# Forming the block sums of a mixing matrix by accumulating DRAM transfers instead of GpSimd adds, in a two-layer attention and gMLP kernel

## The chip, the cores and the metric

The kernel runs on one core of one Trainium2 chip. The metric is the device time of one execution in microseconds (us). Before the change it was measured three times: the median is 1361.53 us, the lowest 1360.88 and the highest 1361.72.

The core has a matrix engine (TensorE, PE in the profile, with its weight loads as PEld), a vector engine (VectorE, DVE), an activation engine (ScalarE, ACT), GpSimd (POOL) and SyncE (SP), which in this kernel only issues DMA transfers. Each engine works off its own instructions in program order: an instruction that waits holds back all that stand behind it on that engine. PEq, SPq and POOLq are the sequencers of these engines, on which their DMA issues are shown.

## What is computed

Two layers, each made of a linear-attention block and a gated mixer block, on 2048 tokens of 512 features, all in float32:

```python
x = x + _A_ref(_layernorm(x), wqkv, wo)                 # linear attention, 32 heads of 16
x = x + _B_ref(_layernorm(x), w_in, w_sp, b_sp, w_out)  # gMLP
x = x + _A_ref(_layernorm(x), wqkv, wo)                 # the same weights again
x = x + _B_ref(_layernorm(x), w_in, w_sp, b_sp, w_out)

# _B_ref
z = gelu(einsum("bsd,df->bsf", x, w_in))                # 2048 x 1792
z1, z2 = z[..., :896], layernorm(z[..., 896:])
g = einsum("ts,bsf->btf", w_sp, z2) + b_sp[None, :, None]
return einsum("bsf,fd->bsd", z1 * g, w_out)

# _A_ref: phi(t) = where(t > 0, t + 1, exp(t)) + 1e-6
num = einsum("bhqd,bhde->bhqe", phi(q), kv)
den = einsum("bhqd,bhd->bhq", phi(q), z)[..., None] + 1e-6
```

The change concerns `w_sp`, the 2048 x 2048 mixing matrix. It depends on no activation, so what is formed from it can be formed at any time.

## The kernel before

**Products.** Every float32 product is made of three matmuls on operands split into a high and a low part (`mm3`, lines 147 to 151; `acc`, lines 1615 to 1621; `nested_mm`, lines 1550 to 1553). ACT makes the high part with a copy (`high`, line 135), DVE the low part with a subtraction (`low`, line 138).

**Block sums.** The product with `w_sp` is done by a Strassen-like scheme with seven products in place of eight. It needs, beside blocks of the matrix, four sums of blocks: S1 = A21 + A22, S3 = A21 + A11, S2 = S1 + A11 and S4 = S2 + A12. Each block has 8 row slabs k (0 to 7), and each slab two halves j of 128 x 512 numbers (256 KB). The sums are kept in DRAM, one tile `s{m}_{k}` of 512 KB for each sum m and slab k, 32 tiles in all. They are made once, during layer one, and read in both layers by `P4.fetch` (line 1415) ahead of the products P6 (S2), P7 (S3), P5 (S1) and P3 (S4).

**How they are made.** The class `Sums` does it half slab by half slab: 16 first units (three raw pieces are loaded by SP, GpSimd makes three adds at line 1209, three sums are stored at line 1202) and 16 fourth units (S2 and A12 are loaded, one add, one store). That is 64 adds of 128 x 512. `TOKEN_TICKS` puts seven of the first units into the steps of `P2.run` (SP loads into z tiles of which the tag is free, line 1195; SP stores), and `MIX_TICKS` puts the other 25 units into the mixing steps of `P4.run` (SP loads into page slots, GpSimd issues the stores).

**Order of the work in layer one.** The order is written out by hand:
- `P1.first`, steps s = 1 to 17: layer norm, K and Q projections and the matrix G for each of 16 token tiles.
- `transition`, the change of halves: the attention's small matrices, and the first token tiles of the next part (`p2.a(0)` to `p2.a(3)`, line 793, a multiplication on GpSimd; `a2_den` on DVE at line 805; `a2_mul` at line 814).
- `P2.run`, steps s = 1 to 18: the attention output (`c`, DVE add `c2` at line 846), the second layer norm, its turning through DRAM, and the two halves of `w_in` (`e` and `f`).
- `P4.run`, steps g = 0 to 61: the mixing products (`mm`), each step fetching the matrix part of step g + 4.
- then the output projection, which runs into layer two.

**The norm of a token tile in `P2.run`.** `c_stats` takes the statistics on DVE (lines 264 and 266). GpSimd makes rs and nb of them in three small instructions (lines 268, 269, 273). `c3` normalises on ACT (line 279) with nb. On ACT the late part of phi(q) stands behind that (lines 417 and 418), on DVE its last instruction (line 419), and behind this on DVE the add `c2` (line 846), the low part of the next token tile (line 138) and the statistics of the tile after (264, 266). A token tile's attention operand (`qt`) goes to DRAM and comes back rearranged (SP, lines 315 and 131), and DVE transposes it in 32 x 32 blocks (line 330).

**Queues.** All loads and nearly all stores are issued by SP, in program order. Each of SP's DMA issues also waits until the eighth issue before it has landed, and GpSimd's are guarded in the same way among themselves.

## Time and profile before

| | |
|---|---|
| median of three runs | 1361.53 us |
| time of the profiled execution | 1361.72 us |
| its span, first to last instruction | 1360.0 us (1.72 us lie around it) |
| PE busy | 1353.4 us |
| DVE busy | 1034.1 us |
| ACT busy | 638.1 us |
| POOL busy | 496.3 us |
| PE's granted clock | 1.00 throughout |
| bytes moved by DMA | 310.18 MB, 228 GB/s on the mean |

How to read the views: a row of a timeline gives the start in us from the span's start, the duration in us, engine, source line, operation, the tile written and the tiles read by their program names without numbers, and in brackets how long the engine had been idle before and what ended that. "x4" merges four in a row. A row of the waits gives the waiting instruction, what it waited for, then the total in us, the number of times and the longest. A row of stretches gives the busy time of each engine with its number of instructions, then PE's clock, the share of time in which the 16 DMA engines were busy, and what they moved. A row of DMA issues ends with the number of issues, the size of each and the median time from issue to landing. "L1202" is line 1202 of the kernel before. In the changed kernel lines below the edits have other numbers: 793 becomes 806, 846 becomes 859, 1202 and 1204 are the new transfers.

### The profile page before, as it was taken

To read this page: it belongs to the slowest core of one execution; us is meant where nothing else is said; L and a number is where in the kernel's file an instruction comes from. 1 tells how busy PE (TensorE), PEld (TensorE's weight loads), DVE (VectorE), ACT (ScalarE), POOL (GpSimd) and SP (SyncE) were. 2 spreads that over 40 slices of the span, in tenths; PEclk is the share of its full clock that TensorE was granted. 3 is DMA by queue.
4 is the path that set the end of the run, shared out by engine and by line. 5 is a ranking of instruction groups with operands and counts; after the bars stand their busy time and mean duration, and the time that the engine had idled before them with its cause. 6 is when DMAs were issued, how large, how long until landed. Compare 5 with 4: busy or idle time off the path is not lost.

```text
span 1360.0 us, 18353 instructions
## 1 busy us (share of the span) xinstructions
PE 1353.4 (100%) x6087; PEld 1133.3 (83%) x6087; DVE 1034.1 (76%) x1582; ACT 638.1 (47%) x1021; POOL 496.3 (36%) x594
## 2 busy tenths in 40 slices
PE   9999999999999999999999999999999999999998
PEld 7888888888888888888888888888888888888887
DVE  7985898776866789985678768877768798978642
ACT  6875544446443342532456655443556434533310
POOL 2333376533284248427321134533230011412340
PEclk9999999999999999999999999999999999999999
DMA  5773478976797988886876524666568798568652
GB/s 182 238 210 93 124 263 295 303 238 186 235 353 266 310 285 277 265 345 201 252 227 214 178 83 127 203 220 204 187 205 278 225 335 318 198 200 304 224 184 88
DMA packets 181744, 310.18 MB, mean 228 GB/s; under 512 B 15696, under 2 KB 67920, under 8 KB 177552
## 3 DMA queue, kind: packets, MB, share of 16 engines
q1 hardware_dynamic: 166544, 251.45, 57.1%
q0 software_dynamic: 11504, 51.12, 10.4%
q10 hardware_dynamic: 3600, 6.42, 1.3%
q8 instruction: 48, 0.79, 0.2%
q14 instruction: 48, 0.39, 0.1%
HBM read 211.68 MB, written 97.26 MB: 227 GB/s over the span
## 4 chain that ended last, share of the span: by engine, by line
PE 95%; DVE 3%; ACT 1%; issue 0%; POOL 0%; DVEq 0%; ACTq 0%; POOLq 0%
PE bank L151 17%; PE bank L149 17%; PE bank L150 17%; PE bank L1620 9%; PE bank L1619 9%; PE bank L1621 9%; PE bank L1552 4%; PE bank L1550 4%; PE bank L1553 4%; PE bank L995 1%; PE bank L994 1%; PE bank L993 1%; PE bank L736 1%; PE bank L512 0%; DVE pg L138 0%
## 5 line engine op out<-in xcount | busy, mean ns | idle before, releaser
L1621 PE MATMUL bank<-qd,pg 128*128 128x512 f32 x544 | 211.9, 390 | 0.0
L1620 PE MATMUL bank<-qd,pg 128*128 128x512 f32 x544 | 211.9, 390 | 0.0
L1619 PE MATMUL bank<-qd,pg 128*128 128x512 f32 x544 | 211.9, 390 | 0.0
L1466 DVE TENSOR_TENSOR qd<-qd,qd 128x1024 fp32r<-128x1024 f32 x104 | 140.4, 1350 | 65.2 <-ACT qd L1457 64.9
L1457 ACT ACTIVATE qd<-qd 128x1024 fp32r<-128x1024 f32 x104 | 110.1, 1059 | 132.0 <-DMA qd<-s 39.3
L151 PE MATMUL bank<-qd,pg 128*128 128x512 f32 x380 | 148.7, 391 | 0.4 <-DVE pg L138 0.4
L135 ACT ACTIVATE pg<-pg 128x512 fp32r<-128x512 f32 (+1 forms) x146 | 89.4, 620 | 125.0 <-DVE pg L330 46.3
L268 POOL TENSOR_SCALAR rs<-mv 128x1 f32<-128x1 f32 x95 | 42.2, 444 | 260.3 <-DVE mv L266 250.7
L1641 POOL TENSOR_TENSOR bg<-bg,pg 128x512 f32<-128x512 f32 x56 | 89.8, 1614 | 108.2 <-DMA pg<-z 98.8
L1620 PEld LDWEIGHTS bank<-qd,pg 128*128 128x128 f32 x544 | 102.2, 188 | 21.2
L1619 PEld LDWEIGHTS bank<-qd,pg 128*128 128x128 f32 x544 | 102.2, 188 | 21.2
L1621 PEld LDWEIGHTS bank<-qd,pg 128*128 128x128 f32 x544 | 102.2, 188 | 21.0
L138 DVE TENSOR_TENSOR pg<-pg,pg 128x512 fp32r<-128x512 f32 (+1 forms) x143 | 106.0, 742 | 16.3 <-ACT pg L135 12.9
L1209 POOL TENSOR_TENSOR pg<-pg,pg 128x512 f32<-128x512 f32 x50 | 80.2, 1604 | 101.9 <-DMA pg<-in_wsp_dram 68.7
L149 PE MATMUL bank<-qd,pg 128*128 128x512 f32 x284 | 111.0, 391 | 0.0
L150 PE MATMUL bank<-qd,pg 128*128 128x512 f32 x284 | 110.7, 390 | 0.0
L330 DVE STREAM_TRANSPOSE pg<-pg 128x512 f32<-128x512 f32 x79 | 86.0, 1089 | 12.7 <-DMA pg<-yt 11.1
L149 PE MATMUL bank<-bg,qd 128*128 128x448 f32 x256 | 94.2, 368 | 0.0
L150 PE MATMUL bank<-bg,qd 128*128 128x448 f32 x256 | 93.7, 366 | 0.0
L151 PE MATMUL bank<-bg,qd 128*128 128x448 f32 x256 | 93.5, 365 | 0.0
L1552 PE MATMUL bank<-qd,pg 128*128 128x512 f32 x224 | 87.5, 391 | 0.3 <-DVE qd L1466 0.3
L1550 PE MATMUL bank<-qd,pg 128*128 128x512 f32 x224 | 87.4, 390 | 0.0
(221 smaller groups left out, 3228.9 us busy)
## 6 DMA issues: line engine op xcount, KB each, us to landing
qd<-s SPq DMA_DIRECT2D x64, 512.0 KB, 4.1
qd<-n POOLq DMA_DIRECT2D x32, 1024.0 KB, 8.1
pg<-in_wsp_dram SPq DMA_DIRECT2D x92, 256.0 KB, 5.0
qd<-in_wsp_dram SPq DMA_DIRECT2D x40, 512.0 KB, 4.4
pg<-z SPq DMA_DIRECT2D x56, 256.0 KB, 4.0
n<-pg SPq DMA_DIRECT2D x55, 256.0 KB, 4.6
x<-pg SPq DMA_DIRECT2D x48, 256.0 KB, 2.8
pg<-x SPq DMA_DIRECT2D x48, 256.0 KB, 3.5
```

Source lines behind the costliest of these rows:

```text
L138: nc.vector.tensor_sub(l, src, h.bitcast(F32))
L149: nc.tensor.matmul(out, ah, bh, start=start, stop=False)
L150: nc.tensor.matmul(out, ah, bl, start=False, stop=False)
L151: nc.tensor.matmul(out, al, bh, start=False, stop=stop)
L1457: nc.scalar.activation(wh, r, AF.Copy)
L1466: nc.vector.tensor_sub(wl, r, wh.bitcast(F32))
L1550: m(out[i], h[:, o, f], w[:, o, 0], start=first and name in ("P1", "P2", "P5"), stop=False, skip_group_check=True)
L1552: m(out[i], h[:, o, f], w[:, o, 1], start=False, stop=False, skip_group_check=True)
L1619: m(out, h[:, o], w[:, 0, j, :], start=start, stop=False, skip_group_check=True)
L1620: m(out, h[:, o], w[:, 1, j, :], start=False, stop=False, skip_group_check=True)
L1621: m(out, l[:, o], w[:, 0, j, :], start=False, stop=stop, skip_group_check=True)
L1641: nc.gpsimd.tensor_tensor(u, u, z1, op=OP.mult)
```

## The change

`Sums` no longer holds tiles in SBUF and makes no add. A sum is formed in DRAM in pairs of stages: an even stage copies one operand from DRAM to the sum's tile (issued by SP), the odd stage after it transfers the other operand onto it with `accum_op=OP.add` (issued by GpSimd). Slab k has six stages: 0 and 1 form S1 and S3 (two transfers each), 2 and 3 form S2 from S1, 4 and 5 form S4 from S2 (one transfer each). That is 4 copies and 4 accumulating transfers a slab, all of 512 KB, 32 and 32 in all. The operands from the matrix lie in DRAM as rows of 2 KB (256 of them); the copies of S1 to S2 and of S2 to S4 go between contiguous tiles (16 rows of 32 KB).

Their places: stages 0 of slabs 0 and 1 at the end of step 16 of `P1.first`, stages 1, 2 and 3 of these slabs behind `p2.a(0)`, `p2.a(1)` and `p2.a(3)` of the transition; from there one stage a step through `P2.run` (slab 2 from step 1 on, even stages at the end of a step, odd ones in its middle), slabs 6 and 7 finished in mixing steps 0 to 5, and stages 4 and 5 of slab k in mixing steps 7 + 3k and 8 + 3k.

On GpSimd's queue the two waiting transfers of stage 3 (slabs 0 and 1) now stand directly ahead of the first rs of `P2.run`, and four accumulating issues stand between `p2.a(0)` and `p2.a(1)`. On SP's queue the two copies of stage 2 stand behind the two `win1` loads of the transition and ahead of a load of x, the first store of x, and the store of the first `qt`; the two copies of stage 0 of slab 2 stand ahead of that `qt`'s load. The instructions of PE, DVE and ACT are the same in kind, number and order.

```diff
-TOKEN_TICKS = {at: (at,) for at in (5, 7, 8, 9, 11, 12, 13)}
-MIX_TICKS = (2, 4, 5, 7, 8, 10, 11, 13, 15, 20, 21, 23, 24, 26, 27, 29, 30, 32, 34, 35, 37, 38, 39, 40, 41)
+TOKEN_SUMS = {s: divmod(s + 7, 4) for s in range(1, NT + 3)}
+MIX_SUMS = {**{g: divmod(g + 26, 4) for g in range(6)}, **{7 + 3 * k + o: (k, 4 + o) for k in range(HT) for o in range(2)}}
...
+                if s == NT:
+                    sums.stage(0, 0)
+                    sums.stage(1, 0)
...
         p2.a(0)
+        if first:
+            sums.stage(0, 1)
+            sums.stage(1, 1)
...
         p2.a(1)
+        if first:
+            sums.stage(0, 2)
+            sums.stage(1, 2)
         p1.late()
...
         p2.a(3)
+        if first:
+            sums.stage(0, 3)
+            sums.stage(1, 3)
...
-                if self.L == 0:
-                    sums.store()
...
-                if self.L == 0:
-                    sums.sum(s, TOKEN_TICKS)
+                if self.L == 0 and s in TOKEN_SUMS and TOKEN_SUMS[s][1] % 2:
+                    sums.at(s, TOKEN_SUMS)
...
-                if self.L == 0 and s + 1 in TOKEN_TICKS:
-                    sums.fetch(TOKEN_TICKS[s + 1])
+                if self.L == 0 and s in TOKEN_SUMS and TOKEN_SUMS[s][1] % 2 == 0:
+                    sums.at(s, TOKEN_SUMS)
...
+        def stage(self, k, n):
+
+            def block(row, at):
+                return wsp_d[row:row + 2, at].rearrange("j p t -> p j t")
+
+            a21, a22, a11, a12 = block(0, k), block(0, k + HT), block(2, k), block(2, k + HT)
+            s1, s2, s3, s4 = (self.s[m, k] for m in range(1, 5))
+            pairs = ((s1, a22), (s3, a21)), ((s1, a21), (s3, a11)), ((s2, s1),), ((s2, a11),), ((s4, s2),), ((s4, a12),)
+            for out, a in pairs[n]:
+                if n % 2:
+                    nc.gpsimd.dma_start(out, a, accum_op=OP.add)
+                else:
+                    nc.sync.dma_start(out, a)
+
+        def at(self, step, stages):
+            if step in stages:
+                self.stage(*stages[step])
...
-                    self.sums.tick(g, MIX_TICKS)
+                    self.sums.at(g, MIX_SUMS)
```

44 lines of the change are left out of this document (1 added, 43 removed).

## The prediction

> **What bounds the kernel now.** I read the busy times first, then PE's waits, then the stretches of the span, and only then the one place where the change puts waits ahead of something urgent.
>
> ```profile
> span 1360.0 us, 18353 instructions
> ...
> PE 1353.4 (100%) x6087; PEld 1133.3 (83%) x6087; DVE 1034.1 (76%) x1582; ACT 638.1 (47%) x1021; POOL 496.3 (36%) x594
> ...
> PE 95%; DVE 3%; ACT 1%; issue 0%; POOL 0%; DVEq 0%; ACTq 0%; POOLq 0%
> ```
>
> PE is busy for 1353.4 of 1360.0 us, and the chain that ended last runs over PE for 95%. Its waits for other engines are these, all of them:
>
> ```profile
> PE bank L512 <- DVE pg L507: 2.0, 1, 2.0
> PE bank L151 <- DVE pg L138: 0.4, 2, 0.2
> PE bank L1552 <- DVE qd L1466: 0.3, 1, 0.3
> ```
>
> The 2.0 us are the first matmul's. L1552 belongs to the mixing of both layers, but nothing of POOL ends any wait of PE. So 0.7 us is the most that the change could win by removing waits, and one of the two 0.2 us waits at L151 lies in its path, below. Does a busy POOL or a busy DMA make PE's own work slower? The stretches compare that:
>
> ```profile
> 374.00:408.00 34.00, 34.00 (x152) 28.17 (x151) 21.76 (x17) 14.65 (x20) 29.69 (x29) 1.00 0.99 353
> 1054.00:1088.00 34.00, 34.00 (x152) 28.17 (x151) 24.02 (x39) 16.59 (x27) 0.00 (x0) 1.00 0.77 225
> ```
>
> With POOL busy 29.69 us and DMA at 0.99, PE does 152 matmuls in 34 us, and as many with POOL at 0.00 and DMA at 0.77. Taking work off POOL wins nothing there. The kernel can hardly become faster; the question is whether it stays as it is.
>
> **What the change removes.** It takes 64 adds off POOL.
>
> ```profile
> L1209 POOL TENSOR_TENSOR pg<-pg,pg 128x512 f32<-128x512 f32 x50 | 80.2, 1604 | 101.9 <-DMA pg<-in_wsp_dram 68.7
> L1202 POOL DMA_DIRECT2D s<-pg x43: 539/557/583, 361.0 to 549.3; - x43
> ```
>
> At 1604 ns each that is 103 us of POOL, and 43 of its store issues at 0.557 us. It counts as 0 in the sum: PE never waited for them. It removes 16 x 6 + 16 x 3 = 144 transfers of 256 KB, 37.7 MB, in place of which come 64 of 512 KB, 33.6 MB, half of them accumulating.
>
> **The price of an accumulating transfer** stands in no row. It goes from DRAM to DRAM, reads two operands and writes one. The nearest rows:
>
> ```profile
> qd<-n POOLq DMA_DIRECT2D x32, 1024.0 KB, 8.1
> ...
> qd<-in_wsp_dram SPq DMA_DIRECT2D x40, 512.0 KB, 4.4
> ...
> pg<-win_sums POOLq DMA_DIRECT2D x24, 256.0 KB, 5.0
> ```
> ```profile
> 368.00:382.00 14.00, 14.00 (x63) 11.61 (x62) 8.11 (x6) 4.67 (x7) 9.10 (x8) 1.00 1.01 364
> ```
>
> Lower end: it costs what a plain transfer of 512 KB on POOL's queue would, a third of the way from 5.0 to 8.1, or 6.0 us to landing, and the next lands 0.524 MB / 364 GB/s = 1.44 us behind it. Upper end: four such times of engine work, 5.8 us apart, the first landing 6.0 + 3 x 1.44 = 10.3 us after its issue. I take the row of 1,024 KB, since that is what it reads: 8.1 us, the next 2.9 us behind. A plain copy within DRAM has no row either; I take 4.4 us for 512 KB, the load's row, and 1.4 us more where it shares the engines with an accumulating one.
>
> The Trainium skill, page "Collectives: The Full Stack", section "The bandwidth ceiling: the fold count and why AG ≠ RS ≠ AR", speaks against this change: an add within the DMA engine costs a second source read on the same ring and halved the rate (measured ratio 1.93). By it the spacing would be 1.93 x 1.44 = 2.8 us and the sum below 0.2 us smaller. No run here shows it yet.
>
> **Where it comes to the path.** The DMA engines are nearly idle at the change of halves, so the transfers there run by themselves:
>
> ```profile
> 130.00:158.00 28.00, 28.00 (x151) 23.94 (x150) 23.58 (x46) 15.09 (x27) 11.39 (x13) 1.00 0.22 66
> ```
> ```profile
> 130.88 5.00 POOL L793 TENSOR_TENSOR pg<-z_q,pg 128x512 f32<-128x512 f32 x4 [2.21 <-ACT pg L720]
> 148.83 0.22 POOL L268 TENSOR_SCALAR rs<-mv 128x1 f32<-128x1 f32 x1 [12.95 <-DVE mv L266]
> ...
> 149.80 0.27 POOL L273 TENSOR_SCALAR nb<-mv,rs 128x1 f32<-128x1 f32 x1
> ...
> 154.89 0.22 POOL L268 TENSOR_SCALAR rs<-mv 128x1 f32<-128x1 f32 x1 [0.93 <-DVE mv L266]
> ```
>
> Between `p2.a(3)` and the first rs POOL has 12.95 us of idle time, and into this gap the change puts a chain of transfers that POOL and SP wait for in turn. Step by step:
> 1. `p2.a(0)` ends at 130.88 + 5.00 / 4 = 132.1. POOL issues S1 and S3 of slab 0, S1 and S3 of slab 1, 4 x 0.557 = 2.2 us; so `p2.a(1)` to `p2.a(3)` end 2.2 us later. DVE reads `p2.a(1)` at 137.02 (row below), and it would now end at 132.1 + 2.2 + 1.25 = 135.6: hidden, with 1.4 us to spare.
> 2. The copies of stage 0 were issued by SP some 17 us before, beside almost no traffic: landed. S1 of slab 0 lands at 132.1 + 8.1 = 140.2, S1 of slab 1, the third, at 140.2 + 2 x 2.9 = 146.0.
> 3. SP has waited for it to issue the copy that starts S2 of slab 1. It lands 4.4 + 1.4 us later, the last accumulating transfer being under way: 151.8.
> 4. POOL has waited for that copy, issues (0.557) and reaches the first rs at 152.4, not 148.83: **3.5 us late**.
>
> Does PE see these 3.5 us? The chain behind rs, row by row:
>
> ```profile
> 150.10 0.81 ACT L279 ACTIVATE pg<-pg,nb,rs 128x512 f32<-128x512 f32 x1 [2.91 <-POOL nb L273]
> ...
> 151.43 0.63 ACT L418 ACTIVATE z_q<-z_q 128x512 f32<-128x512 f32 x1
> ```
> ```profile
> 137.02 0.67 DVE L805 TENSOR_REDUCE den<-pg 128x32 f32<-128x512 f32 x1
> ...
> 152.09 0.69 DVE L419 SCALAR_TENSOR_TENSOR z_q<-bank,z_q 128x512 f32<-128x512 f32 x1 [1.45 <-ACT z_q L418]
> 152.70 0.68 DVE L846 TENSOR_TENSOR pg<-pg,bank 128x512 f32<-128x512 f32 x1
> 153.29 0.69 DVE L138 TENSOR_TENSOR pg<-bank,pg 128x512 fp32r<-128x512 f32 x1
> ...
> 159.06 1.08 DVE L330 STREAM_TRANSPOSE pg<-pg 128x512 f32<-128x512 f32 x1
> ...
> 162.72 0.63 DVE L138 TENSOR_TENSOR pg<-pg,pg 128x512 fp32r<-128x512 f32 x1
> ```
> ```profile
> 154.96 0.39 PE L151 MATMUL bank<-qd,pg 128*128 128x512 f32 x1
> ...
> 163.40 0.50 PE L151 MATMUL bank<-qd,pg 128*128 128x512 f32 x1 [0.24 <-DVE pg L138]
> ```
>
> ACT had waited for nb (2.91 us), DVE for ACT (1.45 us), and DVE then runs without a gap to the low part at 162.72, for which PE waits already. From 152.09 on all of it moves by the delay. PE's first need is at 154.96, with the operand ready at 153.98: 1.0 us of slack. At 163.40 there is none. So of 3.5 us PE sees 2.5 at the first place and the rest at the second: **+3.5 us**.
>
> **SP's queue.** The copies of stage 2 hold SP until 146.0. Behind them stand a load of x, due only at 160.01, the store of x and the `qt` store:
>
> ```profile
> 150.71 0.38 SPq L315 DMA_DIRECT2D qt<-pg  x1
> ...
> 153.20 0.33 SPq L131 DMA_DIRECT2D pg<-qt  x1
> ```
> ```profile
> pg<-qt SPq DMA_DIRECT2D x26, 256.0 KB, 4.1
> ```
>
> SP is free 4.7 us before the `qt` store. Ahead of the `qt` load now stand two copies of 512 KB (2 x 1.4 us, and two issues of 0.33): it lands at 153.2 + 0.7 + 4.1 + 2.8 = 160.8. DVE's transpose of it began at 159.06, so it is 1.7 us late by itself, but behind the 3.5 us of the rs (162.6) it is hidden; if the rs is not late, these 1.7 us come to light.
>
> **The later steps.**
>
> ```profile
> 172.00:298.00 126.00, 126.00 (x586) 109.50 (x585) 103.17 (x172) 53.91 (x90) 77.17 (x103) 1.00 0.86 287
> ...
> 270.00:284.00 14.00, 14.00 (x67) 12.37 (x66) 10.52 (x17) 5.33 (x9) 8.99 (x13) 1.00 0.98 331
> ```
>
> In 172 to 298 us DMA works 0.86 x 126 = 108 us at 287 / 0.86 = 334 GB/s. Seven units of 6 x 256 KB (11.0 MB, 33 us) go; steps 5 to 17 bring 11 copies (5.8 MB, 17 us) and 9 accumulating transfers (4.7 MB, read twice, 28 us): 108 - 33 + 45 = 120 of 126 us, a share of 0.95. At 0.98 PE had no wait (14.00 of 14.00), so I count 0. With the upper price (four times) it is 108 - 33 + 17 + 56 = 148 us, 22 too many. On POOL each pair of issues (1.1 us) and its wait for a copy stands where three adds (4.8 us) stood in seven of the steps. In the mixing steps 25 units become 22 copies and 23 accumulating transfers of half a unit's bytes or less, and POOL has nothing urgent there: 0.
>
> **Sum.** 0 + 3.5 + 0 + 0 on the profiled execution: 1361.72 + 3.5 = 1365.2 us. That run is 0.19 us above the median, so the median becomes 1361.53 + 3.5 = **1365.0 us** (+0.26%).
>
> **Rivals.**
> - *Hidden: not slower.* If an accumulating transfer costs what a plain one does (6.0 us, 1.4 apart), S1 of slab 1 lands at 132.1 + 6.0 + 2.8 = 140.9, the copy at 146.0 or so, POOL is through at 146.6, before 148.83. What is left is the 1.7 us of the `qt` load: 1363.2 us, within 0.2%. It decides where the spacing is below some 2.6 us. For it: DMA at 0.22 in that stretch. Against: two reads.
> - *Slow adds.* At the upper end S1 of slab 1 lands at 132.1 + 10.3 + 11.6 = 154.0, the copy at 159.8, POOL's rs at 160.4: 11.6 us late; SP is held past the `qt` store, and the 22 us by which the DMA engines are short in the later steps come on top: 1361.5 + 34 = 1395 us. Half of that (three reads' worth) gives some 1378. For it: DRAM is read and written at once and nothing shows its rate. Against: nothing either.
> - *Faster.* The 0.2 us wait in the path and 0.3 us of the mixing could go: at most 0.5 us, 1361.0; by over 0.2% only if something that no view shows is at work.
>
> **How the numbers follow.** A difference of 0.2% (2.7 us) is about what a measurement of this kernel can tell from no change. Forecast (an add costs two reads; its own range 1364.3 to 1370) 0.40; hidden, with every small delay of up to 2.7 us, 0.36; slow adds 0.22; faster 0.02. So faster 0.02, same 0.36, slower 0.62. The range goes from 1360.8, all hidden, to 1385, which leaves out the slowest adds (0.15) and the lowest times of the hidden case with the gains (0.04).
>
> **What would show it.** Right: rs of the first token tile 2 to 6 us behind DVE's L266, released by a DMA; PE with a new wait of some 2.5 us near 155 and the rest near 163; the accumulating issues landing near 8 us while the engines are free, and the third of the four some 14 us after its issue; no other wait of PE over 1 us. Wrong: landing near 6 us and POOL idle again until L266 (hidden), or DMA at 1.0 from 172 to 298 us with waits of PE for loads (slow adds), or a `win1` or matrix load held by SP's waits in the mixing, which I priced at 0.

## The result and the profile after

| | before | after |
|---|---|---|
| median | 1361.62 us (4 runs, 1360.88 to 1362.48) | 1386.08 us (4 runs, 1385.26 to 1387.62) |
| time and span of the profiled execution | 1361.72, 1360.0 | 1385.74, 1383.9 |
| PE busy, PE idle within the span | 1353.4, 6.6 | 1363.2, 20.7 |

The changed kernel takes 1.0181 times as long (95% interval 1.0163 to 1.0198), 24.5 us more. Forecast were 1365.0 us, and 1385 at most.

The page of the changed kernel: the span, the busy times, and the chain of work that ended last.

```profile
span 1383.9 us, 18003 instructions
...
PE 1363.2 (99%) x6087; PEld 1135.4 (82%) x6087; DVE 998.0 (72%) x1582; ACT 636.8 (46%) x1021; POOL 404.2 (29%) x519
...
PE 81%; DMA 8%; DVE 5%; ACT 3%; issue 1%; SPq 1%; POOL 0%; ACTq 0%; DVEq 0%; POOLq 0%
```

PE's number of matmuls is the same, and it is busy 9.8 us longer with them; DMA has come into the chain with 8%. The waits of PE in the changed kernel, for whom, with total, number and longest:

```profile
PE bank L149 <- ACT qd L135: 5.9, 5, 2.6
PE bank L151 <- DVE pg L138: 4.0, 3, 2.5
PE bank L512 <- DVE pg L507: 2.0, 1, 2.0
PE bank L1006 <- ACT pg L1014: 1.9, 1, 1.9
PE bank L1006 <- DMA pg<-win_sums: 1.4, 1, 1.4
PE bank L291 <- ACT pg L310: 1.0, 1, 1.0
```

Before, everything behind the first matmul's 2.0 us came to 0.7 us. Now there are eleven more of up to 2.6 us, 14.2 us in these rows. The stretches say where they lie (times are those of the changed kernel; the columns are PE, PEld, DVE, ACT, POOL busy, then PE's clock, the DMA share and GB/s):

```profile
130.00:158.00 28.00, 24.47 (x118) 20.02 (x117) 22.56 (x37) 12.04 (x22) 14.52 (x14) 0.88 0.86 174
186.00:370.00 184.00, 174.60 (x774) 146.26 (x773) 127.89 (x231) 79.22 (x130) 64.93 (x114) 0.98 0.85 244
370.00:600.00 230.00, 230.00 (x1016) 190.52 (x1015) 155.02 (x198) 92.75 (x136) 44.14 (x33) 1.00 0.75 223
```

At the change of halves PE does 118 matmuls, where the kernel before did 151 in the same 28 us, and its granted clock is 0.88. In the token steps (186 to 370 us) it does 774, and the kernel before 843 in as long. From 370 us on nothing is lost.

A second reading of the two traces runs through the whole text below: the start of the same matmul in both, set side by side, gives **PE's delay** against the kernel before at that place. In us, by the time in the kernel before:

| kernel | 141 | 182 | 300.3 | 330 | 340.8 | all of the span |
|---|---|---|---|---|---|---|
| after | 6.6 | 8.2 | 17.7 | 20.5 | 24.2 | 23.9 |
| e1_plain_odd | 3.8 | 4.4 | 4.4 | 4.8 | 8.2 | 7.9 |
| e2_no_halves | -0.1 | 5.3 | 10.5 | 12.4 | 17.0 | 16.7 |
| e3_pairs | 5.4 | 9.1 | 12.2 | 16.2 | 16.2 | 22.4 |
| e4_four_issues | 6.8 | 6.2 | 6.1 | 6.2 | 6.2 | 5.7 |
| e6_one_add | -0.1 | 0.8 | 1.6 | 4.2 | 5.7 | 14.8 |
| e7_issues_last | 0.0 | -0.2 | -0.2 | -0.2 | -0.2 | 0.7 |
| e8_spread | -0.4 | -0.1 | -0.1 | 0.0 | 0.0 | 2.1 |
| e9_all_last | 0.0 | 8.2 | 14.7 | 17.2 | 21.7 | 21.4 |
| e13_split_pairs | 0.2 | 3.3 | 12.4 | 16.8 | 18.8 | 19.4 |
| e14_sparse_pairs | 0.1 | 0.7 | 2.8 | 11.1 | 11.1 | 33.1 |

Each row is of one execution. The times of these versions spread over 1 to 6 us from run to run, and the profiled execution is the slowest of its kernel's in e1, e6, e13 and e14 and the fastest in e2 and e9, so a difference of up to 3 us between two rows is not to be read.

So three losses make up the 24.2 us of the changed kernel: **6.6 us** at the change of halves, **1.6 us** in the first token steps, **16.0 us** in the later token steps. The third has two parts: 12.3 us up to 330 us, and 3.7 us in the last token steps. In the mixing there is none.

**The first loss.** GpSimd, then DVE, then PE at the change of halves, rows of the timeline (start, duration, engine, line, operation, tiles, and in brackets the idle time before and what ended it):

```profile
132.01 4.50 POOL L1202 DMA_DIRECT2D s<-in_wsp_dram  x4
134.56 5.87 POOL L806 TENSOR_TENSOR pg<-z_q,pg 128x512 f32<-128x512 f32 x3
145.57 1.06 POOL L1202 DMA_DIRECT2D s<-in_wsp_dram  x1 [5.15 <-DMA s<-s]
149.93 1.05 POOL L1202 DMA_DIRECT2D s<-in_wsp_dram  x1 [3.29 <-DMA s<-s]
154.58 0.23 POOL L268 TENSOR_SCALAR rs<-mv 128x1 f32<-128x1 f32 x1 [3.61 <-DVE mv L266]
```
```profile
134.55 4.75 DVE L138 TENSOR_TENSOR pg<-pg,pg 128x256 fp32r<-128x256 f32 x1
139.23 1.76 DVE L827 SCALAR_TENSOR_TENSOR pg<-z_q,den 128x512 f32<-128x512 f32 x1
```
```profile
139.36 0.50 PE L151 MATMUL bank<-bg,pg 128*128 128x512 f32 x1 [2.52 <-DVE pg L138]
```

The four issues take 4.50 us, not 2.2. The three multiplications behind them begin at 134.56, beside the end of the issuing, and take 5.87 us, until 140.43; in the kernel before all four were over at 135.88. In the same moment, at 134.55, DVE begins a subtraction of 128 x 256 and is held for 4.75 us; PE waits for its result. The rs of the first token tile, for which the prediction feared GpSimd's waits for transfers, waits for DVE (3.61 us after the last issue).

**The second loss.** DVE's transpose of the first `qt`, and the matmul behind it:

```profile
166.62 1.12 DVE L330 STREAM_TRANSPOSE pg<-pg 128x512 f32<-128x512 f32 x1 [1.99 <-DMA pg<-qt]
```
```profile
171.00 0.51 PE L151 MATMUL bank<-qd,pg 128*128 128x512 f32 x1 [1.16 <-DVE pg L138]
```

**The third loss, first part**, in one token step of the changed kernel: GpSimd's issues of two accumulating transfers; SP's store of a turned tile `yt`, and the load of that tile; DVE's transpose; PE; and the stretches of the store, of the load and behind PE's wait.

```profile
253.24 1.12 POOL L1202 DMA_DIRECT2D s<-in_wsp_dram  x1 [2.19 <-DMA s<-in_wsp_dram]
254.51 1.06 POOL L1202 DMA_DIRECT2D s<-in_wsp_dram  x1 [0.15 <-issue]
```
```profile
251.80 0.37 SPq L315 DMA_DIRECT2D yt<-z_turn  x1
...
257.47 0.39 SPq L131 DMA_DIRECT2D pg<-yt  x1
```
```profile
266.45 1.08 DVE L330 STREAM_TRANSPOSE pg<-pg 128x512 f32<-128x512 f32 x1 [4.10 <-DMA pg<-yt]
```
```profile
268.24 0.47 PE L149 MATMUL bank<-bg,qd 128*128 128x448 f32 x1 [1.80 <-ACT qd L135]
```
```profile
251.80:257.40 5.60, 5.60 (x29) 5.03 (x28) 3.95 (x9) 3.35 (x6) 3.60 (x5) 1.00 1.07 294
257.50:266.40 8.90, 8.90 (x40) 7.11 (x38) 4.71 (x10) 0.63 (x1) 2.57 (x4) 1.00 1.09 291
...
268.00:276.00 8.00, 7.71 (x28) 6.59 (x29) 6.15 (x12) 4.90 (x9) 1.06 (x3) 0.79 0.66 215
```

The load is issued at 257.47, 5.7 us after the store, as soon as that has landed. DVE has its data at 266.45, 9.0 us after that issue; in the kernel before such a load landed after 3.3 us in the median and 4.8 at most. During the store and the load the DMA engines are busy all the time (1.07 and 1.09). DVE had waited 4.10 us, and PE waits 1.80 us. Then the cost grows: in the next 8 us PE is busy for 7.71, but at a granted clock of 0.79 it does 28 matmuls, where the kernel before did 38 to 40 in every 8 us around this time. PE's 9.8 us of extra busy time go with such stretches. Each of the five waits of PE at L149 (5.9 us) stands behind a transpose that was released by its load of a `yt`.

**The third loss, second part**, in the last token steps, on GpSimd:

```profile
351.99 1.12 POOL L1202 DMA_DIRECT2D s<-in_wsp_dram  x1 [6.19 <-DMA s<-in_wsp_dram]
355.23 1.04 POOL L1202 DMA_DIRECT2D s<-in_wsp_dram  x1 [2.12 <-DMA s<-in_wsp_dram]
356.35 0.23 POOL L268 TENSOR_SCALAR rs<-mv 128x1 f32<-128x1 f32 x1
...
357.83 1.73 POOL L988 DMA_DIRECT2D pg<-win_sums  x3 [0.24 <-issue]
```

Two accumulating issues wait for their copies (6.19 and 2.12 us). Behind them stand the rs of the last token tile, for whose normalisation ACT waits and behind it ACT's copy at L1014, and the loads of `win_sums` (sums of blocks of `w_in`, kept in DRAM). PE waits for both: 1.91 us at 359.30 and 1.37 us at 365.06, the two rows of L1006 above. This is the chain that the prediction followed at the change of halves, in another place.

### The profile page after: what moved, and what is told of

Read it like the earlier page. It is cut to its first block, busy times and chain, and to the rows that moved or that the text cites. A ratio compares the mean times of both kernels' runs of the same rounds, so it can differ in the third digit from the quotient of the medians.

```text
span 1383.9 us, 18003 instructions
## 1 busy us (share of the span) xinstructions
PE 1363.2 (99%) x6087; PEld 1135.4 (82%) x6087; DVE 998.0 (72%) x1582; ACT 636.8 (46%) x1021; POOL 404.2 (29%) x519
## 3 DMA queue, kind: packets, MB, share of 16 engines
q0 software_dynamic: 16768, 56.63, 15.9%
## 4 chain that ended last, share of the span: by engine, by line
PE 81%; DMA 8%; DVE 5%; ACT 3%; issue 1%; SPq 1%; POOL 0%; ACTq 0%; DVEq 0%; POOLq 0%
PE bank L151 13%; PE bank L149 13%; PE bank L150 13%; PE bank L1596 9%; PE bank L1597 9%; PE bank L1598 9%; PE bank L1529 3%; PE bank L1530 3%; PE bank L1527 3%; DMA pg<-yt 2%; DMA yt<-z_turn 2%; DMA pg<-qt 1%; DVE pg L330 1%; PE bank L1006 1%; DVE pg L138 1%
## 5 line engine op out<-in xcount | busy, mean ns | idle before, releaser
L1443 DVE TENSOR_TENSOR qd<-qd,qd 128x1024 fp32r<-128x1024 f32 x104 | 135.4, 1302 | 97.5 <-ACT qd L1434 96.7
L1598 PEld LDWEIGHTS bank<-qd,pg 128*128 128x128 f32 x544 | 102.1, 188 | 21.4
L1596 PEld LDWEIGHTS bank<-qd,pg 128*128 128x128 f32 x544 | 102.1, 188 | 21.3
L1597 PEld LDWEIGHTS bank<-qd,pg 128*128 128x128 f32 x544 | 102.1, 188 | 20.9
L138 DVE TENSOR_TENSOR pg<-pg,pg 128x512 fp32r<-128x512 f32 (+1 forms) x143 | 108.1, 756 | 14.8 <-ACT pg L135 14.2
L149 PE MATMUL bank<-qd,pg 128*128 128x512 f32 x284 | 110.9, 390 | 0.0
L149 PE MATMUL bank<-bg,qd 128*128 128x448 f32 x256 | 96.0, 375 | 5.9 <-ACT qd L135 5.9
L151 PE MATMUL bank<-bg,qd 128*128 128x448 f32 x256 | 95.1, 371 | 0.3
L150 PE MATMUL bank<-bg,qd 128*128 128x448 f32 x256 | 94.8, 371 | 0.0
L151 PEld LDWEIGHTS bank<-qd,pg 128*128 128x128 f32 x380 | 71.5, 188 | 19.2 <-DVE pg L138 4.3
```

The costliest lines, as they stand in the source:

```text
L138: nc.vector.tensor_sub(l, src, h.bitcast(F32))
L149: nc.tensor.matmul(out, ah, bh, start=start, stop=False)
L150: nc.tensor.matmul(out, ah, bl, start=False, stop=False)
L151: nc.tensor.matmul(out, al, bh, start=False, stop=stop)
L1443: nc.vector.tensor_sub(wl, r, wh.bitcast(F32))
L1596: m(out, h[:, o], w[:, 0, j, :], start=start, stop=False, skip_group_check=True)
```

## The experiments

Theory 1: an accumulating transfer costs the DMA engines about two plain ones, and those that stand in the token steps make the round trips of `yt` and `qt` late; apart from it, the four issues at the change of halves hold DVE. Theory 2: it is GpSimd's (and SP's) waits for transfers, behind which their other work stands.

### e1_plain_odd: no adding

```diff
-                    nc.gpsimd.dma_start(out, a, accum_op=OP.add)
+                    nc.gpsimd.dma_start(out, a)
```

> All transfers, places and waits of the changed kernel, but the odd stages are plain transfers from GpSimd's queue: the sums lack their second operand, so the output is not that of the reference. Theory 1 (the loss behind 190 us comes from the DMA engines, which read twice for an add): the delay of PE between 190 and 370 us, 16 us in the changed kernel, falls to under 5 us. Theory 2 (it comes from POOL and SP standing in wait for the stage before): it stays near 16 us less what the shorter landings save, so 8 us or more. At the change of halves: if the hold of DVE (4.75 us for one L138) comes from writing descriptors for an add, it goes, and the issue falls from 1.1 us towards 0.56; if it comes from 256 rows, both stay. Theory 1 with the hold kept: 1361.6 + 7 + 4 = 1373 us; with the hold gone: 1367 us. Theory 2: 1377 us or more.

Measured: 1366.89 us, 1.0041 times before (1.0026 to 1.0056). The two transfers side by side, first the changed kernel, then this one (queue, packets, MB, share; and number, size, median us to landing):

```profile
q0 software_dynamic: 16768, 56.63, 15.9%
...
s<-in_wsp_dram POOLq DMA_DIRECT2D x32, 512.0 KB, 8.5
```
```profile
q0 software_dynamic: 12672, 56.63, 12.2%
...
s<-in_wsp_dram POOLq DMA_DIRECT2D x32, 512.0 KB, 5.9
```

The same bytes take 15.9% of 1383.9 us, or 12.2% of 1367.9 us: 53 us of all 16 engines, 1.66 us for each of the 32 adds. Of the first part of the third loss 0.4 us are left (delay 4.4 at 182, 4.8 at 330; 12.3 us in the changed kernel). The second part stays, 3.4 us. Meanwhile GpSimd waits for transfers longer than in the changed kernel (18.3 + 17.9 us between 186 and 370 us, there 16.2 + 2.2):

```profile
POOL s L1202 <- DMA s<-in_wsp_dram: 18.3, 8, 7.5
POOL s L1202 <- DMA s<-s: 17.9, 2, 16.0
```

So up to 330 us the waits are there and cost next to nothing: for the first part theory 2 fails and theory 1 holds. For the second part it is the other way round. Two of these waits (7.49 us until 336.83 and 1.90 until 339.43) stand ahead of the last token tile's rs and of the loads of `win_sums`, as in the changed kernel, and PE waits 1.39 us at 343.12 and 1.47 at 349.01: what costs there, by these rows, is GpSimd's wait for the copies, whether it adds or not. Of the first loss 3.8 us stay (DVE's L138 is held for 4.41 us by plain issues too), so most of it is not the price of adding.

### e2_no_halves: nothing at the change of halves

```diff
-TOKEN_SUMS = {s: divmod(s + 7, 4) for s in range(1, NT + 3)}
+TOKEN_SUMS = {s: divmod(s - 1, 4) for s in range(1, NT + 3)}
...
-                    sums.stage(0, 0)
-                    sums.stage(1, 0)
```

(The calls in the transition go as well, and the mixing steps take up what is moved later.)

> The same 32 copies and 32 adds, but nothing at the change of halves: slabs 0 to 4 go one stage a step through the 18 steps of P2.run, slabs 4 to 7 through mixing steps 0 to 13, stages 4 and 5 into mixing steps 14 to 29. If POOL's issue of four adds at once makes the 6.6 us at the change of halves, PE has no wait near 139 us and the time falls by 6 to 8 us to 1379 us. If the 24 us are one common shortage of DMA time over the whole of layer one, the time stays at 1384 to 1388 us, only shifted in place.

Measured: 1380.36 us, 1.0142 (1.0125 to 1.0158). The delay is -0.1 at 141 us: the first loss comes from what stands at the change of halves. From 182 to 340.8 us 11.7 us are lost, so the third does not hang on it. The second loss is larger, 5.4 us against 1.6: the second `qt` store, issued at 158.42, now lands after 9.5 us (2.5 before), its load is issued only at 168.00, and PE waits 1.45 us at 172.77 and 1.80 at 175.30.

### e3_pairs: two slabs in turn

```diff
-TOKEN_SUMS = {s: divmod(s + 7, 4) for s in range(1, NT + 3)}
+ORDER = [(2 + 2 * (i // 8) + i % 2, i % 8 // 2) for i in range(24)]
+TOKEN_SUMS = {s: ORDER[s - 1] for s in range(1, NT + 3)}
```

> As the changed kernel, but from step 1 of P2.run on the stages of two slabs alternate, so that each stage has two steps, not one, between it and the stage that it waits for; the transfers, their number a step and the DMA bytes are the same. Theory 1 (DMA engines): the delay of PE between 190 and 370 us stays at 12 to 18 us, the time at 1383 to 1387 us. Theory 2 (POOL and SP held by waits between stages): the waits of POOL and SP for transfers of s go, the delay falls to under 5 us, the time to 1374 us.

Measured: 1384.21 us, 1.0170 (1.0155 to 1.0185). GpSimd's waits for transfers between 186 and 370 us fall from 18.4 to 3.2 us, and the time by less than 2 us. Up to 330 us 7.1 us are lost (12.3 in the changed kernel) though hardly a wait is left: with e1 this is against theory 2 for the first part, from both sides. The second part is gone (0.0 us from 330 to 340.8), as theory 2 wants it there. In its place some 6 us are lost at the start of the mixing, where four accumulating issues stand between 348.9 and 356.3 us and a load of a matrix part lands only 13.7 us after its issue.

### e4_four_issues and e7_issues_last: the first loss by itself

Both are the kernel before with four copies and four accumulating transfers into tiles that nobody reads. They differ in the place of GpSimd's four issues, `extra(1)`:

```diff
         p2.a(0)
+        if p1.L == 0:        # e4_four_issues
+            extra(1)
...
         p2.a(3)
+        if p1.L == 0:        # e7_issues_last
+            extra(1)
```

> The kernel before, with only this added at the change of halves: four copies of 512 KB into spare DRAM tiles at the end of step 16 of P1.first, and behind p2.a(0) four accumulating transfers from GpSimd onto them, for which nothing waits. If the issue alone holds DVE: one L138 near 134 us takes some 4.7 us, PE waits 3 to 4 us near 139 us with its clock below 1.00 behind it, and the time is 1361.6 + 6.5 = 1368 us. If it takes the chain of waits behind it (stages 2 and 3), the time stays within 2 us of the kernel before, 1361.6 to 1363.5 us.

> The kernel before with four copies and four accumulating transfers into spare tiles that nobody reads, as in the run with four issues, but with GpSimd's four issues behind its fourth multiplication of the change of halves and not behind the first. Theory 1 (writing the descriptors of a transfer holds DVE, whatever GpSimd does beside it): a DVE instruction that starts between 135 and 141 us takes over 3 us again, PE waits 1 us or more, 1364 to 1368 us. Rival (DVE was held by GpSimd's multiplications, which ran slower beside the issues): no DVE instruction is held over 1.5 us, 1361.4 to 1363 us.

Measured: e4 1367.37 us, 1.0041 (1.0027 to 1.0055), with the very loss of the changed kernel (delay 6.8 at 141 us, DVE's L138 4.76 us long); e7 1361.07 us, 0.9996 (0.9987 to 1.0006). In e7 GpSimd's multiplications are over when it issues, and DVE's two subtractions are as short as in the kernel before (0.84 and 0.41 us there too):

```profile
135.83 4.50 POOL L710 DMA_DIRECT2D spare<-in_wsp_dram  x4
```
```profile
135.35 0.84 DVE L138 TENSOR_TENSOR pg<-pg,pg 128x256 fp32r<-128x256 f32 x1
...
136.72 0.41 DVE L138 TENSOR_TENSOR pg<-pg,pg 128x256 fp32r<-128x256 f32 x1
```

The four transfers and their issues cost nothing there, and DVE runs on beside the 4.50 us of issuing. Theory 1 as written for e7 (writing descriptors holds DVE) fails; the multiplications behind the issues are what counts.

### e10_one_each, e11_two_issues, e12_pool_delay: what holds DVE

e10 sets one of the four issues behind each multiplication, e11 has two issues behind the first. e12 has no transfer, but other work of GpSimd in their place:

```diff
         p2.a(0)
+        if p1.L == 0:
+            d = small.tile([P, 8], F32, name="delay", bufs=1)
+            nc.gpsimd.memset(d, 1.0)
+            for _ in range(6):
+                nc.gpsimd.tensor_scalar(d, d, 1.0, 0.0, op0=OP.mult, op1=OP.add)
```

> The kernel before with the four copies and four accumulating transfers into spare tiles of the run with four issues, the four issues set one behind each of GpSimd's four multiplications of the change of halves. Theory 1 (a multiplication of GpSimd that stands behind issues waits until their descriptors are written, and an instruction of DVE that starts meanwhile waits with it, so the hold grows with the issues in front): up to three DVE instructions are longer by at most about 1.2 us each, the loss is 0 to 3 us, 1361.5 to 1364.5 us. Rival (a hold of about 4 us follows any issue with a multiplication behind it): one or more DVE instructions of over 3 us, 1366 us or more.

> The same, with two issues only, both behind the first multiplication (four copies, two accumulating transfers). Theory 1: the DVE instruction at the first multiplication behind the issues is held by about half of what it was (1.5 to 2.5 us in place of 4.8), PE sees 0 to 2 us: 1361.5 to 1364 us. Rival (the hold does not depend on the number): 4 us or more, 1366 us or more.

> The kernel before, with seven small instructions of GpSimd on a spare tile of 128 x 8 (one fill, six scalings) between its first and its second multiplication of the change of halves, and no transfer. They hold back the second to fourth multiplication by some 1.6 to 3 us, as the issues did. Theory 1 (the issues matter only because the multiplications then run beside another instruction of DVE): a DVE instruction is held over 3 us and PE waits over 1 us: 1363.5 to 1367 us. Rival (a multiplication that stands behind DMA issues is what holds DVE): no DVE instruction from 133 to 141 us is longer than 1.5 us, and the time is within 0.1% of the kernel before, 1361 to 1363 us.

Measured: e10 1363.94 us, 1.0017 (1.0008 to 1.0027), DVE's two subtractions 2.66 and 1.50 us, the time as theory 1 had it, the first hold longer; e11 1365.16 us, 1.0024 (1.0015 to 1.0034), with a loss between the two expected; e12 1362.96 us, 1.0010 (1.0000 to 1.0020). GpSimd and DVE in e11:

```profile
133.78 4.73 POOL L810 TENSOR_TENSOR pg<-z_q,pg 128x512 f32<-128x512 f32 x3
```
```profile
134.05 4.51 DVE L823 TENSOR_TENSOR den<-den,zeps 128x32 f32<-128x32 f32 x1
```

and in e12:

```profile
133.76 4.45 POOL L798 TENSOR_TENSOR pg<-z_q,pg 128x512 f32<-128x512 f32 x3
```
```profile
135.29 1.77 DVE L819 SCALAR_TENSOR_TENSOR pg<-z_q,den 128x512 f32<-128x512 f32 x1
136.99 1.50 DVE L138 TENSOR_TENSOR pg<-pg,pg 128x256 fp32r<-128x256 f32 x1
```

In e11 it is a tiny operation, 128 x 32 and 0.19 us long in e12, that lasts 4.51 us: until 138.56, where GpSimd's third multiplication ends (138.51). In e12 the multiplications begin at the same 133.76, and DVE is held three times by about one multiplication: 0.81, 1.77 and 1.50 us, where the same three took 0.84, 0.68 and 0.41 in the kernel before. There the multiplications met, a little earlier, the operation of 128 x 32 (0.87 us in place of 0.19). So the later multiplications alone put DVE's next reduction from 137.02 to 138.41, 1.4 us, and cost the kernel 1.2 us (my theory there missed, and its rival too, by a little). Behind transfer issues one operation of DVE is held much longer: in e11 through all three multiplications, in the changed kernel until 139.30, when the third was still under way (until 140.43), and there the operation behind it is held too (1.76 us). The hold hardly grows from two issues to four (4.51 and 4.75 us), against what I had expected of e11. Why DVE does not get in between the multiplications when issues went before is not shown by any view; so that the issues lengthen the hold is shown, and by what is not.

### e9_all_last: the changed kernel with its issues moved

```diff
         p2.a(3)
         if first:
-            sums.stage(0, 3)
-            sums.stage(1, 3)
+            for n in range(1, 4):
+                sums.stage(0, n)
+                sums.stage(1, n)
```

(The calls behind `p2.a(0)` and `p2.a(1)` go.)

> The changed kernel, with the accumulating issues of stage 1 and the copies of stage 2 moved behind the fourth multiplication of the change of halves, so that stages 1, 2 and 3 of slabs 0 and 1 stand there one behind the other. Theory 1 with the chain of the prediction: DVE is not held near 134 us (no loss of 6.6 us there), but GpSimd now comes to the first rs only some 19 us after the four issues, near 155 us in place of 148.8, so PE sees 4 to 6 us there: 1382 to 1386 us in all. Rival (the chain of waits is harmless): GpSimd idle again until L266, 1378 to 1380 us. If the hold at 134 us does not go away, 1386 us or more.

Measured: 1385.63 us, 1.0178 (1.0164 to 1.0192). This is what theory 1 expected. DVE is not held, the delay at 141 us is 0.0, and at 182 us it is 8.2 all the same:

```profile
153.96 1.03 POOL L1197 DMA_DIRECT2D s<-in_wsp_dram  x1 [3.90 <-DMA s<-s]
155.06 0.23 POOL L268 TENSOR_SCALAR rs<-mv 128x1 f32<-128x1 f32 x1
```
```profile
157.21 1.12 PE L291 MATMUL bank<-ident,pg 128*128 128x128 f32 x4 [5.74 <-ACT pg L279]
```

The rs now stands right behind the last issue, 6.2 us later than before (148.83), and PE waits 5.74 us for the normalised tile behind it. This is the chain that the prediction described. In the changed kernel it was hidden behind the hold of DVE; with the hold gone it takes its place.

### e5_one_layout: long rows

```diff
-            self.s = {(m, k): dram.tile([P, 2, 512], F32, name=f"s{m}_{k}") for m in range(1, 5) for k in range(HT)}
+            self.s = {(m, k): dram.tile([2, P, 512], F32, name=f"s{m}_{k}") for m in range(1, 5) for k in range(HT)}
...
-                    nc.gpsimd.dma_start(out, a, accum_op=OP.add)
+                    nc.gpsimd.dma_start(out, a, accum_op=OP.add, max_dma_last_dim=8192)
```

(`block` and `P4.fetch` are turned to suit.)

> The changed kernel, with the tiles of the sums in DRAM kept in the order of the matrix (two halves of 128 rows each, one behind the other), so that both operands and the result of every transfer lie in one piece: the 256 rows of 2 KB of an accumulating transfer become 64 of 8 KB, and the copies become long rows. Bytes, places and number of transfers are the same. Theory 1 (an accumulating transfer is dear because it reads two operands): the share of the DMA engines from 181 to 316 us stays near 0.89, the loss there stays, and only the loss at the change of halves may shrink: 1380 to 1387 us. Rival (it is dear because of its many short rows): GpSimd's issue falls from 1.1 us towards 0.4, landing from 8.5 us to 6 or less, the DMA share from 181 to 316 us to 0.8 or less, and the time to 1363 to 1373 us.

Measured: 1660.59 us, 1.2194 (1.2175 to 1.2214), which no theory had. GpSimd's issues of stage 1 wait for the copies of stage 0, which SP had issued from 113.57 us on:

```profile
138.76 1.11 POOL L1202 DMA_DIRECT2D s<-in_wsp_dram  x1 [5.35 <-DMA s<-in_wsp_dram]
151.51 1.09 POOL L1202 DMA_DIRECT2D s<-in_wsp_dram  x1 [11.63 <-DMA s<-in_wsp_dram]
```

They, and the next at 164.26, are released 12.75 us apart, 512 KB each, 41 GB/s, with the DMA engines busy for 0.33 of the time from 114 to 170 us. The copies, not the adds, became the bound, so the run doesn't tell whether short rows make an add dear. That a copy of two long pieces is spread over few of the 16 engines would explain it; this was not tried.

### e6_one_add and e8_spread: fewer in the token steps

e6 gives each step one transfer of one sum, 18 in the token steps in place of 28 and none at the change of halves; e8 does its eight at the change of halves with the issues behind `p2.a(3)`, then one in each of token steps 1 to 14 and one in each of mixing steps 0 to 41:

```diff
+ORDER = [(k, n) for k in range(2) for n in (4, 5)]
+ORDER += [(k, n) for k in range(2, HT) for n in (0, 1, 4, 5)]
+ORDER += [(k, n) for k in range(2, HT) for n in (2, 3)] + [(k, n) for k in range(HT) for n in (6, 7)]
+TOKEN_SUMS = {s: ORDER[s - 1] for s in range(1, 15)}
+MIX_SUMS = {g: ORDER[g + 14] for g in range(len(ORDER) - 14)}
...
+            pairs = ((s1, a22),), ((s1, a21),), ((s3, a21),), ((s3, a11),), ((s2, s1),), ((s2, a11),), ((s4, s2),), ((s4, a12),)
```

> The changed kernel, with one transfer in each step and none at the change of halves: only S1 and S2 are formed from step 1 of the token part to mixing step 13 (copy, add, copy, add for each slab), S3 in mixing steps 13 to 21, S4 from mixing step 23 on. In the 18 token steps there are then 9 copies and 9 accumulating transfers. Theory 1 (work of the DMA engines): by the prices of the prediction 6.5 copies and 6.5 adds in steps 5 to 17 are 30 us of engine work in place of the 33 us of the units removed, so the token part shows no new wait: 1362 to 1367 us. Rival (every accumulating transfer that stands ahead of the loads of yt and qt holds them by its landing, whatever the load): at least half of the loss from 190 to 340 us stays, 1370 to 1376 us. Loss in the mixing (more transfers there than in the changed kernel): 0 by theory 1, since no wait was seen there; 3 us or more if the load of the mixing counts.

> A version put together from the runs so far: the eight transfers of S1 and S3 of slabs 0 and 1 stay at the change of halves, their accumulating issues behind the fourth multiplication, where they cost nothing; then one transfer a step, of a single sum each, in token steps 1 to 14 only, none in steps 15 to 18, and one a step in mixing steps 0 to 41. Theory 1 (the loss is engine work ahead of urgent loads in crowded stretches, and the hold of GpSimd and DVE behind the four issues): no wait of PE over 1 us, DMA share at most 1.0 in the mixing, 1361.5 to 1366 us. Rival (accumulating transfers hold loads by themselves, at any density): 1368 us or more, with waits for yt and qt in the token part.

Measured: e6 1374.20 us, 1.0084 (1.0067 to 1.0101); e8 1364.14 us, 1.0026 (1.0014 to 1.0039). In e6 the delay is 1.6 us at 300 and 5.7 at the end of the token part, so that part does what theory 1 says until its last steps; but the mixing, where two transfers a step now stand in eight steps, loses 9 us at one place, against theory 1, which put that at 0. So the time lies in the rival's range, for another reason than the rival's. The stretch:

```profile
420.00:480.00 60.00, 52.99 (x229) 43.20 (x228) 30.09 (x42) 17.45 (x24) 9.29 (x9) 0.96 1.03 297
```
In it PE waits 6.8 us at one place, and the load of a sum on the chain to this wait landed 15.4 us after its issue (4.1 in the median of the kernel before).

e8, with at most one a step, has a DMA share of 0.93 from 370 to 600 us, no delay at 340.8 us, and 2.1 us at the end, which arise from 580 us on (one wait of PE of 1.06 us there, just over the 1 us of theory 1). It is the fastest of the versions with accumulating transfers throughout, and still slower than the kernel before.

### e13_split_pairs and e14_sparse_pairs: how many, or how close

e6 and e8 have fewer transfers in the token steps and none in pairs. e13 is e2 with the two transfers of a stage half a step apart, e14 has about as few as e6, but in pairs in every second step.

```diff
-                if self.L == 0 and s in TOKEN_SUMS and TOKEN_SUMS[s][1] % 2:
-                    sums.at(s, TOKEN_SUMS)
+                if self.L == 0 and s in TOKEN_SUMS and TOKEN_SUMS[s][1] != 2:
+                    sums.stage(*TOKEN_SUMS[s], slice(0, 1))
```
```diff
+TOKEN_SUMS = {1 + 2 * i: (i // 2, i % 2) for i in range(9)}
```

> The run without transfers at the change of halves, with the same transfers in the same steps, but the two transfers of a stage for S1 and S3 no longer issued together: the first in the middle of the step, the second at its end. In that run PE's matmuls lose 11.7 us between 182 and 341 us. If the loss comes from two accumulating transfers standing together ahead of an urgent load (pairing), it falls to 4 us or less, and the time to 1372 us or less. If it comes from how many there are in the token part (28 of 512 KB), it stays at 9 to 13 us: 1377 to 1383 us.

> The opposite trial: as few transfers in the token steps as in the run with one a step (10 copies and 8 accumulating ones), but always two together, in every second step; nothing at the change of halves; the rest two a step in mixing steps 0 to 11 and one a step to mixing step 32. Read by PE's delay between 182 and 341 us, which is 4.9 us there. If pairing decides, the delay gained there is 8 us or more; if the number decides, 3 to 6 us. What the crowded mixing steps lose comes on top and is read apart: 1368 to 1380 us in all.

Measured: e13 1379.09 us, 1.0125 (1.0105 to 1.0144), of which 15.5 us arise between 182 and 341 us (11.7 in e2); the medians are within 1.3 us: taking the pairs apart saves nothing that shows. e14 1393.86 us, 1.0231 (1.0214 to 1.0248), slower than either answer had it, with 22 us of it in the crowded mixing. Between 182 and 300 us e14 loses 2.1 us (e6 0.8), then 8.3 us more, nearly all at one place:

```profile
302.10 2.21 POOL L1195 DMA_DIRECT2D s<-in_wsp_dram  x2
```
```profile
303.25 0.37 SPq L319 DMA_DIRECT2D yt<-z_turn  x1
312.03 0.32 SPq L135 DMA_DIRECT2D pg<-yt  x1
```
```profile
316.70 0.74 PE L153 MATMUL bank<-bg,qd 128*128 128x448 f32 x1 [5.79 <-ACT qd L139]
```
```profile
303.30:311.90 8.60, 7.61 (x36) 6.41 (x35) 5.36 (x12) 3.05 (x5) 3.12 (x7) 1.00 0.96 184
```

Two accumulating transfers are issued from 302.10 on, SP's store of `yt` in the middle of them at 303.25, and its load, for which SP waits until the store has landed, is issued only at 312.03, 8.8 us later. PE waits 5.79 us. While the store is under way the DMA engines are busy for 0.96 of the time, but move 184 GB/s, where the kernel before moved 331 at 0.98 (270 to 284 us). So neither the number nor the pairing is the cause by itself, and e14 came out on the side of pairing only by this one place.

What the versions have in common is no trial, but it can be counted from the rows of their timelines: the twelve round trips of `yt` in layer one, in each of the eight versions with adds in the token steps (the changed kernel, e2, e3, e6, e8, e9, e13, e14).

| accumulating transfers under way meanwhile (GpSimd's issue to landing) | 0 | 1 | 2 |
|---|---|---|---|
| load of `yt`, issue to landing, median us (number) | 3.3 (57) | 5.5 (30) | 7.8 (8) |
| whole trip, issue of the store to landing of the load | 7.8 (45) | 9.8 (32) | 13.0 (18) |

One more load, with four under way, took 8.3 us and its trip 13.0. In the kernel before the twelve loads took 3.2 us in the median and the trips 8.0. Whether a late trip costs anything hangs on how early the tile is needed. At the trip that starts near 250 us PE waits where it took 13.9 us or more (0.6 us in e2 and e9, 1.8 in the changed kernel, 2.7 in e13) and not where it took 13.2 or less (e1, e3, e6, e8, e14). Near 300 us trips of 10.6 to 11.6 us already cost 2.2 to 5.8 us. e1's longest trip, near 245 us, took 12.6. So what makes the first part of the third loss is accumulating transfers under way during the round trip of a tile that has little time to spare; the more there are, the later it is. What the runs leave open is how the engines share out their time between the queues.

## Why the prediction was wrong, point by point

1. *No gain from the 103 us of adds taken off POOL.* Right: no version is faster. e8, in which GpSimd adds nothing either and PE has no delay up to 340.8 us, is not ahead of the kernel before at any place by more than 0.8 us.
2. *The price of an accumulating transfer, 8.1 us to landing and 2.9 us of engine time.* Right in size: 8.5 us in the median, and 1.66 us of engine time more than a plain one. At the change of halves the four landed 3.1 us apart on the mean (138.60 to 147.77 us), in e1 the four plain ones 1.3 (137.38 to 141.41). A plain one takes about 1.55 us, an estimate from e1's row of that queue (12.2% of 1367.9 us for 56.63 MB), so an adding one takes 3.2. The Trainium skill's page "Collectives: The Full Stack", section "The bandwidth ceiling: the fold count and why AG ≠ RS ≠ AR", has a measured ratio of 1.93 between a collective that copies and one that adds. The trace roughly agrees: 3.2 to 1.55 makes 2.1, an estimate.
3. *Step 1, "hidden, with 1.4 us to spare".* Failed, 6.6 us (3.8 without the adding in e1). An accumulating issue by itself took 1.1 us and not the 0.557 us of the store row. But the multiplications began only 2.5 us later, near the 2.2 of the prediction; what failed is that they then took 5.87 us and held an instruction of DVE for 4.75. The prediction asked only when `p2.a(1)` would be ready for DVE, not which of DVE's instructions GpSimd would hold meanwhile. e7 shows that the same issues behind the multiplications are free.
4. *Steps 2 to 4, the chain through stage 2 to the rs, +3.5 us.* The landing times were right within 2 us (S1 of slab 0 at 138.60, forecast 140.2; of slab 1 at 145.19, forecast 146.0; GpSimd through at 150.98, forecast 152.4), but the cost was not seen here, since the rs was late for DVE's sake until 154.58. That the chain is real is shown by e9: rs at 155.06, PE waits 5.74 us. The 3.5 us themselves were never put to the test in the changed kernel.
5. *The `qt` load, 1.7 us late by itself.* Right: DVE waited 1.99 us for it and PE 1.16. It came to light because the rs, 5.75 us later than before, was not late for a PE that was itself 6.6 us late.
6. *The later steps at a DMA share of 0.95, "at 0.98 PE had no wait so I count 0".* The load was right, the conclusion failed, and this is the largest error, 16.0 us. The prediction has 120 us of engine work; measured are 0.89 x 135 us = 120 us between 181 and 316 us. But a mean over 135 us doesn't tell whether the engines are free when an urgent round trip needs them. In the example the share is 1.07 and 1.09 during the trip and 0.66 right after it, and the load took 9.0 us in place of 3.3; in e14 the store held the load back for 8.8 us. A share of 0.98 without a wait, which the prediction leaned on, was one of plain transfers. That is 12.3 us. The other 3.7 us are GpSimd's wait for a copy, which the prediction names in this step ("its wait for a copy") and puts at nothing: 6.19 and 2.12 us ahead of the last token tile's rs.
7. *Mixing steps: 0.* Right for the changed kernel. The count was wrong: there are 12 copies and 12 accumulating transfers in these steps, not 22 and 23, and the sum does not hang on it. e6 shows the bound: 1.03 over 60 us, and 9 us are lost.
8. *Not in the sum:* after some of the short waits PE's clock falls: 0.79 over the 8 us from 268 us on, behind a wait of 1.80, but 1.00 from 171 to 179 us, behind one of 1.16. Of the extra 23.9 us of span 14.1 are idle time of PE (20.7 against 6.6) and 9.8 are longer busy time for the same matmuls, which goes with the lower granted clock.

The rival "slow adds" (1378 to 1395 us) had the right time by the wrong price: it wanted adds of three or four plain transfers' worth. They are worth about two, and the late round trips, the hold of DVE and GpSimd's waits do the rest.

## What to carry to other kernels

A transfer of which nobody waits for the result can still cost the path: look for round trips through DRAM (a store, and a load that waits for it) in the same stretch, and ask how many transfers, and how long ones, can be under way beside each half; a mean DMA share below 1 over many steps says nothing of that. An engine that waits for one transfer before it issues the next keeps all its later work waiting: look for the one instruction behind it that is urgent, also in the last step of a part. When an engine's instructions are pushed back by DMA issues, check not only when their results are due but which instructions of the other engines they will now run beside. And where PE has no slack, count more than the wait itself: here 14.1 us of idle time became 23.9.

## What the runs showed of the hardware that was not expected

- A DVE operation with an operand pair in SBUF was held by GpSimd's multiplications until one was over (1.77 and 1.50 us in e12), and behind DMA issues for longer (4.51 us, until all three were over, for an operation of 0.19 us in e11; 4.75 us in the changed kernel). The issuing itself did not hold it (0.68 and 0.41 us beside 4.50 us of issuing in e7, as in the kernel before).
- An accumulating issue of 256 rows took GpSimd 1.1 us, a plain one of the same rows 0.7 us (4.50 us for four in a row, 2.91 in e1).
- A load of 256 KB took 3.3, 5.5 and 7.8 us in the median with none, one and two accumulating transfers of 512 KB under way.
- Behind PE waits of 2.52 and 1.01 us its clock was 0.69 over 8 us (142 to 150), behind one of 1.80 us 0.79, behind one of 1.16 us 1.00.
- Copies of 512 KB in two long pieces landed 12.75 us apart in e5, those of 16 rows of 32 KB in the changed kernel 5.3 us after their issue.
